# Longer row chunks in the channel mix, another way to turn the inverse row sums, and a re-tuned instruction order, in a top-k attention and channel-mix kernel

## The chip, the core and the metric

The kernel runs on one core of a Trainium2 chip. The metric is device time in microseconds of one launch. Before the change the median of three runs is 1353.63 us (1351.79 to 1354.52).

## What is computed

For 8 batches, 8 heads, 576 positions and a head size of 64, attention keeps for each row only the scores that reach the row's 32nd largest one, and normalises their exponentials by the row's sum plus 1e-9. The 4608 rows of 512 attention outputs then go through a channel mix with a gate:

```python
kth = np.partition(scores, -top_k, axis=-1)[..., -top_k:-top_k + 1]
scores = np.where(scores >= kth, scores, -1000000000.0)
attn = np.exp(scores - np.max(scores, axis=-1, keepdims=True))
attn = attn / (np.sum(attn, axis=-1, keepdims=True) + 1e-09)
x = np.matmul(attn, v)                       # then laid out as (8, 576, 512)
xk = mu_k * x + (1.0 - mu_k) * x_prev        # x_prev is x one row earlier, zeros for the first
xr = mu_r * x + (1.0 - mu_r) * x_prev
k = np.maximum(xk @ w_k, 0.0)                # 512 -> 1024
out = 1.0 / (1.0 + np.exp(-(xr @ w_r))) * (k * k @ w_v)   # gate 512 -> 512, value 1024 -> 512
```

Everything is float32. The channel mix keeps its accuracy by splitting each operand into a high and a low part of a faster format, so every product there is three matmuls (high by high, high by low, low by high).

## The kernel before

**Attention.** The work is cut into 288 tiles of 128 query rows by 576 keys: 32 pairs of heads (a batch and two heads), nine tiles each, of which the ninth holds the last 64 rows of both heads. A tile is scored on TensorE (L878, L882), copied to SBUF on ScalarE (L887), and its top 24 scores are found on VectorE, in seven pieces of 82 or 83 columns (L891, L893, L896). ScalarE's sign (L911), GpSimd's product (L913) and VectorE (L914, L916) find the 32nd score. ScalarE takes the exponential (L919); VectorE masks it and sums the rows in one pass (L922). TensorE then transposes the tile (L928, L937), ScalarE copies the transposes out (L930, L939), and TensorE multiplies by the values (L959, L961).

**Inverse row sums.** Four tiles of a pair form a unit (the ninth tile is a unit of its own), so there are 64 units of four tiles and 32 of one. When the last tile of a unit is masked, VectorE adds 1e-9 to the unit's row sums in place in SBUF (`inv`, L967) and takes the reciprocal (`inv2`, L968). The reciprocals stand one per partition, and they are needed along the free axis. TensorE does that turn with ordinary float32 matmuls: the reciprocal, broadcast to 64 columns, is the stationary operand and an identity the moving one (`turni`, L975), four matmuls for a unit of four tiles and two for a unit of one. The trace shows each of these as two instructions. ScalarE copies the result from PSUM to the tile `ri` (L981, L985), and VectorE multiplies the unit's sums by it into `xT`, the input of the channel mix (`place`, L992, L994).

**Channel mix.** The 4608 rows are taken in 22 chunks: 14 of 256 rows and 8 of 128 (the list `SIZES`). For each chunk GpSimd and ScalarE build the mixed inputs. Then TensorE computes the hidden layer (8 blocks of 128 hidden units, 4 pieces of the inner dimension, 3 products: 96 matmuls in the chunk, whose moving operand has as many columns as the chunk has rows), the gate (12 matmuls of 512 columns for each tile of up to 128 rows) and the value (24 matmuls of 512 columns for each such tile). Lines L597, L598 and L599 are the three products of one helper that serves all of these.

**PSUM.** Four banks, the `rot` tiles, take turns for everything that TensorE hands to another engine: transposed queries, keys and tiles, the inverse's turn, the hidden layer, the gate and the value. Two banks hold the scores and, at their outer ends, the unit's sums; the last two hold the exponentials and small tables.

**Order.** Every engine runs a list in order. The lists are made by a planner in the kernel (`Plan.run`), a list scheduler: each operation has a cost and a latency in nanoseconds, written by hand beside it, a key (its tile number plus an offset of its kind from `OFF`), and the tiles that it reads and writes. The planner walks through time, gives each engine the operation with the lowest key among those that can start within `NEAR` of the first, and grants a PSUM bank with the first operation that touches it. It knows extra costs on TensorE for going from one kind of work to another (`SWITCH`, `LEAVE`). Keys of the channel mix follow from the chunk's rows, `LAG`, `STEP`, `GATE` and `VALUE`. The emitted program is that list; at run time engines wait for one another by semaphores.

**Start.** VectorE, ScalarE and GpSimd first also turn the weights, which come as float64, into their high and low parts (L1158 to L1167), between the first attention tiles. The first matmul of the channel mix starts at 133.9 us.

Of the kernel before, what the change touches and what calls it, by code (L numbers as in the profile page):

```python
# [12 lines left out]
U32 = mybir.dt.uint32  # L13
AF = mybir.ActivationFunctionType
# [23 lines left out]
OFF = dict(kt=-7.052, kq=-6.285, rest=-4.016, v=-5.966, v8=-9.546, tk=-5.123, ck=-4.93, tq=-4.175, cq=-3.66, tr=-3.125, cr=-1.859, zero=7.516,  # L38
           score=-0.127, score8=0.064, keep=0.192, cand=1.258, best=1.414, drop=1.347, under=2.182, nb=-0.455, count=2.757, below=0.194, eighth=2.792,
           nine=1.785, exps=3.38, mask=2.98, turn=4.142, et=4.225, turnl=4.186, el=3.09, weigh=3.203, inv=2.807, inv2=4.903, turni=1.271, ri=4.531,  # L40
           place=4.604, lowest=26.228, ranks=3.686, mu=-1.636, nmu=1.291, changek=0.194, sharek=1.657, addk=-4.799, xhk=-4.813, xlk=-5.803,
           changer=-5.066, sharer=-4.564, addr=-3.661, xhr=-2.482, xlr=-2.503, hidden=0.91, relu=-0.32, sq=0.517, r2=-0.381, hl=-0.874, gate=2.195,
           gexp=1.225, ga=0.235, ln=1.619, inv1=1.333, newton=-1.097, value=0.746, scaled=-2.837, gated=-1.729, store=1.13, w=4.163, wabs=-1.596,
           wclamp=-0.639, wshift=-2.64, wsign=-0.217, wexp=-0.626, wfine=-1.896, whi=0.301, wmul=1.745, wsub=2.282, wlo=-0.346)
# [11 lines left out]
NEAR = dict(PE=128, ACT=137, DVE=15, POOL=110, SP=236)  # L56
# [82 lines left out]
class Plan:  # L139
# [53 lines left out]
    def run(self):  # L193
# [57 lines left out]
        while left:  # L251
            best = None
            for lane in lanes:
# [11 lines left out]
                t, item = min(((t, item) for t, item in able if t <= first + NEAR[lane]), key=lambda x: (x[1][0].key, x[1][0].n))  # L265
# [50 lines left out]
def topk_attention_channel_mix(ctx: ExitStack, tc: tile.TileContext, q, k, v, mu_k, mu_r, w_k, w_v, w_r, out):  # L316
# [448 lines left out]
    def attend(plan, visits, X, pair_sums):  # L765
# [8 lines left out]
        for p, (b, hp, part) in enumerate(visits):  # L774
# [84 lines left out]
            for i in part:  # L859
# [451 lines left out]
```

## Time and profile before

| | |
|---|---|
| median of three runs | 1353.63 us |
| the profiled execution's own time | 1351.31 us |
| its span, first to last instruction | 1349.5 us |
| busy: TensorE matmul | 1266.5 us, 94% |
| busy: VectorE | 1183.4 us, 88% |
| busy: ScalarE | 1148.0 us, 85% |
| busy: GpSimd | 986.7 us, 73% |
| mean granted TensorE clock | 0.969 of 2.4 GHz |

PE is TensorE, DVE VectorE, ACT ScalarE, POOL GpSimd. The profile counts a matmul as busy from its start to its modelled end, and matmuls overlap in the pipeline: one takes about 280 ns and the next can start 110 ns later. What a matmul costs its engine is therefore read from the distance between two starts in the timeline, not from its duration.

### The profile page before, as it was taken

How to read it: one execution, taken by the hardware profiler on the slowest of the kernel's cores; microseconds unless marked ns; L12 is line 12 of the kernel's file. 1: busy time of each engine (PE TensorE's matmuls, PEld its weight loads, DVE VectorE, ACT ScalarE, POOL GpSimd, SP SyncE). 2: the span in 40 equal slices, each digit the busy share in tenths (PEclk: the TensorE clock that was granted, in tenths of full speed). 3: DMA queues.
4: the chain of work that ended last, by engine and by line, in shares of the span. 5: the costliest groups of instructions: out<-in, count | busy, mean ns of one | idle time of the engine just before them, and what ended most of it. 6: DMA issues, size and time to landing. Idle time of an engine off the chain costs nothing.

```text
span 1349.5 us, 33121 instructions
## 1 busy us (share of the span) xinstructions
PE 1266.5 (94%) x10417; PEld 971.0 (72%) x10417; DVE 1183.4 (88%) x6220; ACT 1148.0 (85%) x2552; POOL 986.7 (73%) x858
## 2 busy tenths in 40 slices
PE   6566999999999989999999999999999999999996
PEld 3344777777777867777777777777877777777985
DVE  7999999998899899999899999999999999996000
ACT  7788899988899799989899899989799899987342
POOL 4998977766777568767688686867688687868584
PEclk9666999999999999999999999999999999999999
DMA  6532223223112121211221112111211213221000
GB/s 177 145 98 79 48 55 74 53 67 72 47 35 49 35 55 38 53 40 46 48 49 42 49 42 49 40 50 31 57 45 34 56 43 76 52 59 45 20 15 25
DMA packets 223386, 73.96 MB, mean 55 GB/s; under 512 B 216033, under 2 KB 216033, under 8 KB 223201
## 3 DMA queue, kind: packets, MB, share of 16 engines
q1 hardware_dynamic: 222656, 71.62, 21.5%
q8 instruction: 85, 1.39, 0.4%
q14 instruction: 101, 0.82, 0.2%
q10 hardware_dynamic: 544, 0.13, 0.0%
HBM read 62.26 MB, written 9.44 MB: 53 GB/s over the span
## 4 chain that ended last, share of the span: by engine, by line
PE 54%; DVE 30%; ACT 9%; issue 2%; POOL 2%; SPq 0%; DMA 0%; DVEq 0%; ACTq 0%; POOLq 0%
PE rot L597 9%; PE rot L599 9%; PE rot L598 9%; DVE cand L891 7%; PE ps L878 7%; PE rot L928 6%; DVE E L922 6%; PE ps L959 5%; DVE top L914 4%; PE rot L975 3%; DVE top L893 2%; DVE cand L896 2%; PE rot L831 2%; ACT sc L887 2%; ACT sg L911 2%
## 5 line engine op out<-in xcount | busy, mean ns | idle before, releaser
L913 POOL TENSOR_TENSOR sg<-sc,sg 128x576 f32<-128x576 f32 x288 | 408.0, 1419 | 217.3 <-ACT sg L911 214.0
L891 DVE MAX8 cand<-sc 128x8 f32<-128x82 f32 (+1 forms) x2016 | 406.3, 233 | 8.4 <-ACT sc L887 7.4
L911 ACT ACTIVATE sg<-sc,seen 128x576 f32<-128x576 f32 x288 | 224.5, 780 | 23.5 <-DVE seen L903 20.2
L922 DVE SCALAR_TENSOR_TENSOR E<-sc,seen,se 128x576 f32<-128x576 f32 x288 | 231.2, 803 | 1.4 <-ACT se L919 0.8
L919 ACT ACTIVATE se<-sc,seen 128x576 f32<-128x576 f32 x288 | 215.7, 749 | 13.6 <-DVE E L922 9.0
L914 DVE MAX8 top<-sg 128x8 f32<-128x576 f32 x288 | 216.0, 750 | 9.7 <-POOL sg L913 9.1
L878 PE MATMUL ps<-K,qs 64*128 64x288 f32 x1024 | 202.7, 474 | 18.8 <-ACT sc L887 17.7
L928 PE MATMUL rot<-ident,E 128*128 128x128 f32 x1152 | 186.1, 286 | 30.9 <-DVE E L922 14.1
L887 ACT ACTIVATE sc<-ps 128x576 f32<-128x576 f32 x288 | 187.1, 650 | 26.7 <-PE ps L878 17.3
L597 PE MATMUL rot<-xh,wk 128*128 128x256 f32 (+1 forms) x704 | 204.6, 291 | 1.1 <-DVE eb L1127 1.1
L599 PE MATMUL rot<-xh,wk 128*128 128x256 f32 (+1 forms) x704 | 196.2, 279 | 0.0
L598 PE MATMUL rot<-xl,wk 128*128 128x256 f32 (+1 forms) x704 | 196.0, 278 | 0.0
L928 PEld LDWEIGHTS rot<-ident,E 128*128 128x128 f32 x1152 | 132.6, 145 | 79.9 <-DVE E L922 21.6
L893 DVE MAX8 top<-cand 128x8 f32<-128x56 f32 x864 | 179.8, 208 | 4.2
L930 ACT ACTIVATE et<-rot 128x512 f32<-128x512 f32 x288 | 171.7, 598 | 4.8 <-PE rot L928 4.4
L959 PE MATMUL ps<-et,v 128*64 128x128 f32 x2048 | 146.8, 285 | 0.3 <-ACT et L930 0.2
L597 PEld LDWEIGHTS rot<-xh,wk 128*128 128x128 f32 x704 | 134.8, 191 | 7.5 <-issue 5.0
L959 PEld LDWEIGHTS ps<-et,v 128*64 128x64 f32 x2048 | 116.6, 141 | 30.6 <-issue 16.1
L598 PEld LDWEIGHTS rot<-xl,wk 128*128 128x128 f32 x704 | 134.0, 190 | 0.2
L599 PEld LDWEIGHTS rot<-xh,wk 128*128 128x128 f32 x704 | 133.6, 190 | 0.0
L878 PEld LDWEIGHTS ps<-K,qs 64*128 64x128 f32 x1024 | 80.4, 192 | 65.0 <-issue 28.5
L1096 POOL TENSOR_TENSOR r<-r 128x512 f32<-128x512 f32 (+1 forms) x88 | 77.9, 886 | 63.2 <-ACT hh L1094 56.5
(103 smaller groups left out, 2895.3 us busy)
## 6 DMA issues: line engine op xcount, KB each, us to landing
kt<-in_k SPq DMA_DIRECT2D x192, 72.0 KB, 2.2
v<-in_v SPq DMA_DIRECT2D x92, 128.0 KB, 2.5
kq<-in_q SPq DMA_DIRECT2D x80, 128.0 KB, 2.5
out<-eb SPq DMA_DIRECT2D x36, 256.0 KB, 2.1
kq<-in_q SPq DMA_DIRECT2D x94, 64.0 KB, 2.1
stage<-in_moe_w_k SPq DMA_DIRECT2D x8, 512.0 KB, 4.7
vu<-in_v SPq DMA_DIRECT2D x32, 128.0 KB, 2.4
stage<-in_moe_w_v SPq DMA_DIRECT2D x8, 512.0 KB, 3.7
```

What stands on the lines that cost most here:

```text
L597: nc.tensor.matmul(ps, lhsT=sh, rhs=mh, start=first, stop=False)
L598: nc.tensor.matmul(ps, lhsT=sh, rhs=ml, start=False, stop=False)
L599: nc.tensor.matmul(ps, lhsT=sl, rhs=mh, start=False, stop=last)
L878: nc.tensor.matmul(ps.t[:, e * HS:(e + 1) * HS], lhsT=P.qs[j].t[h, c * 128:(c + 1) * 128], rhs=P.K.t[h, j], start=True, stop=True)
L891: lambda T=T, c=c: nc.vector.max(T.cand.t[:, 8 * c:8 * c + 8], T.sc.t[:, CUTS[c]:CUTS[c + 1]]), reads=[T.sc], writes=[(T.cand, c)])
L911: lambda T=T, sn=sn: nc.scalar.activation(T.side.t, T.sc.t, AF.Sign, bias=sn(T, 1), scale=-BELOW, accum_out=T.top.t[:, TOPK:TOPK + 1]),
L913: plan.op(POOL, "below", n, 1375, 1430, lambda T=T: nc.gpsimd.tensor_mul(T.side.t, T.sc.t, T.side.t), reads=[T.sc], writes=[T.side])
L914: plan.op(DVE, "eighth", n, 660, 754, lambda T=T: nc.vector.max(T.top.t[:, 24:32], T.side.t), reads=[T.side], writes=[(T.top, 3)])
L919: plan.op(ACT, "exps", n, 667, 754, lambda T=T, pe=pe, sn=sn: nc.scalar.activation(pe.t, T.sc.t, AF.Exp, bias=sn(T, 0), scale=SCALE), read ...
L922: lambda T=T, U=U, pe=pe, sn=sn: nc.vector.scalar_tensor_tensor(T.e(), T.sc.t, sn(T, 2), pe.t, op0=OP.is_ge, op1=OP.mult, accum_out=U.rs.t ...
L928: nc.tensor.transpose(pt.t[:, c * 128:(c + 1) * 128], E.t[:, o + c * 128:o + (c + 1) * 128], ident)
L959: nc.tensor.matmul(pa[hs[j]], lhsT=vs[j][:, c, :], rhs=ms[c][j], start=(c == 0), stop=False)
```

## The change

The rows of the channel mix are cut into 19 chunks: fifteen of 256 rows, then 192, 256, 192 and 128. A chunk of 192 rows has a tile of 128 rows and one of 64.

The 1e-9 is added into PSUM instead of in place, and the reciprocal is read from there. GpSimd spreads each reciprocal over 64 columns (128 in a unit of one tile) into `ri`, and TensorE turns that with one or two transposes in place of two or four matmuls. The `rot` bank that takes the turn's result is now the same tile that takes the sum, so it is held from `inv` on. ScalarE's copy and VectorE's product stay as they were.

The planner's numbers are replaced: all offsets in `OFF`, `STEP`, `GATE`, `VALUE`, `NEAR` and others; several costs (hidden matmuls never under 111.7 ns, the weights' `wexp` 850 in place of 400, `ln` 650 in place of 537); more kinds of switch on TensorE; and `BONUS`, which shifts the key of a TensorE operation by the kind of work that came before it. `SPREAD` is "POOL", so the branches for ScalarE are not taken.

```diff
-SIZES = [256, 256, 128, 128, 256, 128] + [256, 256, 128, 256, 256] * 2 + [256, 256, 128, 128, 256, 128]
+SIZES = [256] * 15 + [192, 256, 192, 128]
-LAG, STEP, WAT, WSTEP, GATE, VALUE, PACE = 10.41, 16.746, 0.641, 1.281, 8.0, 12.488, -2.0
+LAG, STEP, WAT, WSTEP, GATE, VALUE, PACE = 10.41, 15.734, 0.542, 1.309, 7.28, 13.747, -2.0
-CANDS, BESTS = 0.062, 0.068
+CANDS, BESTS = 0.078, 0.41
-NEAR = dict(PE=128, ACT=137, DVE=15, POOL=110, SP=236)
+NEAR = dict(PE=158, ACT=176, DVE=0, POOL=131, SP=28)
+SPREAD, PLACE2 = "POOL", 340
...
-                t, item = min(((t, item) for t, item in able if t <= first + NEAR[lane]), key=lambda x: (x[1][0].key, x[1][0].n))
+                t, item = min(((t, item) for t, item in able if t <= first + NEAR[lane]), key=lambda x: (x[1][0].key + BONUS.get((mode, x[1][0].mode), 0.0), x[1][0].n))
...
-                    plan.op(DVE, "inv", n, 55, 150, lambda U=U: nc.vector.tensor_scalar(U.rs.t[:, :U.w], U.rs.t[:, :U.w], 1e-9, None, op0=OP.add), writes=[U.rs])
-                    plan.op(DVE, "inv2", n, 76, 170, lambda U=U: nc.vector.reciprocal(U.rs.t[:, :U.w], U.rs.t[:, :U.w]), writes=[U.rs])
-                                nc.tensor.matmul(pr.t[h, u * 128:(u + 1) * 128], lhsT=s.to_broadcast([128, 64]), rhs=ident, start=True, stop=True)
+                    plan.op(DVE, "inv", n, 60, 155, lambda U=U, pr=pr: nc.vector.tensor_scalar(pr.t[:, :U.w], U.rs.t[:, :U.w], 1e-9, None, op0=OP.add), reads=[U.rs], writes=[pr])
+                    plan.op(DVE, "inv2", n, 76, 170, lambda U=U, pr=pr: nc.vector.reciprocal(U.rs.t[:, :U.w], pr.t[:, :U.w]), reads=[pr], writes=[U.rs])
+                    each = 64 if i < 8 else 128
...
+                        to, r = U.ri.t[:, :w * each].rearrange("p (w d) -> p w d", w=w), U.rs.t[:, :w, None].to_broadcast([128, w, each])
+                            nc.gpsimd.tensor_scalar(to, r, 1.0, 1.0, op0=OP.mult, op1=OP.mult)
...
+                        for u in range(m):
+                            nc.tensor.transpose(pr.t[:, u * 128:(u + 1) * 128], U.ri.t[:, u * 128:(u + 1) * 128], ident)
...
-                    piece("hidden", key(f + e), 12 * (10.7 + n * 0.418), hid, [xh, xl, *[(X.w["k"], (i, f // 4)) for i in range(HP)]], [ph])
+                    piece("hidden", key(f + e), 12 * max(111.7, 10.7 + n * 0.418), hid, [xh, xl, *[(X.w["k"], (i, f // 4)) for i in range(HP)]], [ph])
```

## Rows read from the trace of the kernel before

**Rows 1.** The page: busy time of each engine with its share of the span and its instructions, and the shares of the engines in the chain of work that ended last.
```profile
PE 1266.5 (94%) x10417; PEld 971.0 (72%) x10417; DVE 1183.4 (88%) x6220; ACT 1148.0 (85%) x2552; POOL 986.7 (73%) x858
...
PE 54%; DVE 30%; ACT 9%; issue 2%; POOL 2%; SPq 0%; DMA 0%; DVEq 0%; ACTq 0%; POOLq 0%
```

**Rows 2.** The windows view: five stretches of the span. After the stretch and its length stand the busy times of PE, PEld (weight load), DVE, ACT and POOL with their instructions, then the granted TensorE clock, the DMA engines' share and GB/s.
```profile
0.00:70.00 70.00, 44.04 (x230) 26.86 (x232) 61.82 (x251) 51.40 (x106) 46.70 (x47) 0.76 0.60 158
70.00:240.00 170.00, 145.19 (x1156) 105.96 (x1157) 167.43 (x833) 150.77 (x332) 140.28 (x112) 0.87 0.29 72
240.00:1200.00 960.00, 939.76 (x8010) 720.35 (x8010) 909.99 (x4937) 870.61 (x1945) 701.12 (x601) 1.00 0.20 48
1200.00:1260.00 60.00, 59.42 (x534) 48.48 (x532) 36.70 (x191) 40.55 (x98) 37.55 (x37) 1.00 0.20 51
1260.00:1349.00 89.00, 78.06 (x496) 69.30 (x494) 7.51 (x13) 34.61 (x75) 61.02 (x64) 0.97 0.05 17
```

**Rows 3.** Groups of instructions by line and shape, TensorE: busy time and mean duration of one, idle time before. "128x256" is a chunk of 256 rows.
```profile
L928 PE MATMUL rot<-ident,E 128*128 128x128 f32 x1152 | 186.1, 286 | 30.9 <-DVE E L922 14.1 <-DVE top L893 4.3 <-ACT wv L1164 3.6
L597 PE MATMUL rot<-xh,wk 128*128 128x256 f32 x448 | 133.5, 298 | 1.1 <-DVE eb L1127 1.1
L597 PE MATMUL rot<-wv,hh 128*128 128x512 f32 x288 | 122.2, 424 | 0.0
L597 PE MATMUL rot<-xh,wk 128*128 128x128 f32 x256 | 71.1, 278 | 0.0
L597 PE MATMUL rot<-wr,xh 128*128 128x512 f32 x144 | 61.6, 428 | 0.1
L975 PE MATMUL rot<-ident,rs 128*64 128x128 f32 x640 | 56.6, 289 | 14.2 <-DVE rs L968 8.9 <-DVE top L893 1.4 <-DVE least L1001 1.3
```

**Rows 4.** Timeline of TensorE: start in the span, time from first start to last end, instructions. First hidden matmuls of 256 columns, from the first of a piece on; then value matmuls of 512 columns; then hidden matmuls of 128 columns. In each gap stand only more matmuls of the same kind: 7 between 1220.05 and 1221.00, 22 between 1265.61 and 1270.97, 43 between 1320.13 and 1325.05.
```profile
1219.61 0.36 PE L597 MATMUL rot<-xh,wk 128*128 128x256 f32 x1
1219.81 0.28 PE L598 MATMUL rot<-xl,wk 128*128 128x256 f32 x1
1220.05 0.28 PE L597 MATMUL rot<-xh,wk 128*128 128x256 f32 x1
...
1221.00 0.28 PE L599 MATMUL rot<-xh,wk 128*128 128x256 f32 x1
...
1265.61 0.40 PE L597 MATMUL rot<-wv,hh 128*128 128x512 f32 x1
...
1270.97 0.39 PE L599 MATMUL rot<-wv,hl 128*128 128x512 f32 x1
...
1320.13 0.28 PE L597 MATMUL rot<-xh,wk 128*128 128x128 f32 x1
...
1325.05 0.28 PE L599 MATMUL rot<-xh,wk 128*128 128x128 f32 x1
```

**Rows 5.** Timeline of TensorE around the inverse's turn (L975) and around transposes (L928, L937).
```profile
701.39 0.66 PE L975 MATMUL rot<-ident,rs 128*64 128x128 f32 x8 [0.80 <-DVE rs L968]
701.98 0.66 PE L928 MATMUL rot<-ident,E 128*128 128x128 f32 x4
...
709.49 0.60 PE L928 MATMUL rot<-ident,E 128*128 128x128 f32 x4
710.02 0.76 PE L878 MATMUL ps<-K,qs 64*128 64x288 f32 x4
...
1223.25 0.28 PE L599 MATMUL rot<-xh,wk 128*128 128x256 f32 x1
1223.37 0.60 PE L928 MATMUL rot<-ident,E 128*128 128x128 f32 x4
1223.80 0.27 PE L937 MATMUL rot<-ident,E 128*128 128x128 f32 x1
...
1225.21 0.28 PE L599 MATMUL rot<-xh,wk 128*128 128x256 f32 x1
1225.42 0.66 PE L975 MATMUL rot<-ident,rs 128*64 128x128 f32 x8
1225.90 1.04 PE L959 MATMUL ps<-et,v 128*64 128x128 f32 x16
```

**Rows 6.** Groups by line and shape, VectorE: the sum with 1e-9 of four and of one column, and the reciprocal of four.
```profile
L967 DVE TENSOR_SCALAR rs<-rs 128x4 f32<-128x4 f32 x64 | 32.8, 513 | 0.0
L968 DVE RECIPROCAL rs<-rs 128x4 f32<-128x4 f32 x64 | 10.3, 160 | 0.0
L967 DVE TENSOR_SCALAR rs<-rs 128x1 f32<-128x1 f32 x32 | 4.5, 140 | 0.0
```

**Rows 7.** Groups by line and shape, GpSimd: the product for the 32nd score, the gate's scalar operation of 512 columns, and a product of 256 columns.
```profile
L913 POOL TENSOR_TENSOR sg<-sc,sg 128x576 f32<-128x576 f32 x288 | 408.0, 1419 | 217.3 <-ACT sg L911 214.0 <-PE rot L599 0.7
L1112 POOL TENSOR_SCALAR eb<-eb 128x512 f32<-128x512 f32 x36 | 69.1, 1920 | 7.3 <-ACT eb L1111 4.8
L1096 POOL TENSOR_TENSOR r<-r 128x256 f32<-128x256 f32 x32 | 19.7, 614 | 33.5 <-ACT hh L1094 31.7 <-PE rot L937 1.2 <-PE rot L599 0.6
```

**Rows 8.** Timeline of VectorE: the sum with 1e-9 of one unit, and the reciprocal that follows it.
```profile
715.28 0.22 DVE L967 TENSOR_SCALAR rs<-rs 128x4 f32<-128x4 f32 x1
...
719.20 0.17 DVE L968 RECIPROCAL rs<-rs 128x4 f32<-128x4 f32 x1
```

More of the change, by code (lines that the diff above doesn't have):

```diff
@@ L37 @@
 BIG = 3.0e38
[L38 to L44, printed above, removed]
@@ L45 @@
-CANDS, BESTS = 0.062, 0.068
-LAG, STEP, WAT, WSTEP, GATE, VALUE, PACE = 10.41, 16.746, 0.641, 1.281, 8.0, 12.488, -2.0
+OFF = dict(kt=-7.011, kq=-6.835, rest=-7.805, v=-6.026, v8=-9.812, tk=-4.608, ck=-4.01, tq=-4.295, cq=-5.669, tr=-2.503, cr=-5.25, zero=7.982,
+           score=-0.504, score8=-2.241, keep=-0.323, cand=3.327, best=-1.159, drop=-0.827, under=-0.596, nb=-0.484, count=2.034, below=1.029,
+           eighth=2.875, nine=4.624, exps=2.951, mask=3.076, turn=3.921, et=4.228, turnl=3.656, el=1.141, weigh=3.297, inv=-0.082, inv2=5.091,
+           turni=1.833, ri=3.642, place=5.157, lowest=22.268, ranks=1.808, mu=-4.015, nmu=5.336, changek=7.504, sharek=-2.362, addk=-8.89, xhk=-4.232,
+           xlk=-11.512, changer=-0.97, sharer=-0.964, addr=4.74, xhr=-2.376, xlr=-5.331, hidden=0.557, relu=-1.816, sq=1.525, r2=-1.905, hl=-3.093,
+           gate=2.058, gexp=4.068, ga=2.473, ln=-2.445, inv1=2.025, newton=-3.534, value=0.69, scaled=-3.676, gated=-1.387, store=6.538, w=5.489,
+           wabs=-2.2, wclamp=0.087, wshift=-2.193, wsign=0.267, wexp=0.551, wfine=-3.489, whi=1.685, wmul=0.236, wsub=-2.316, wlo=1.183, spread=2.732)
@@ new lines, in attend, with spread @@
+                    plan.op(DVE, "inv2", n, 76, 170, lambda U=U, pr=pr: nc.vector.reciprocal(U.rs.t[:, :U.w], pr.t[:, :U.w]), reads=[pr], writes=[U.rs])
+                    each = 64 if i < 8 else 128
+                    wide = each * w
+                    def spread(U=U, w=w, each=each):
+                        to, r = U.ri.t[:, :w * each].rearrange("p (w d) -> p w d", w=w), U.rs.t[:, :w, None].to_broadcast([128, w, each])
+                        if SPREAD == "POOL":
+                            nc.gpsimd.tensor_scalar(to, r, 1.0, 1.0, op0=OP.mult, op1=OP.mult)
+                        else:
+                            nc.scalar.activation(to, r, AF.Copy)
@@ L976, in attend, with turn_i @@
+                    if SPREAD == "POOL":
+                        plan.op(POOL, "spread", n, 60 + 1.45 * wide, 60 + 1.45 * wide, spread, reads=[U.rs], writes=[U.ri], mode="TS")
+                    else:
+                        plan.op(ACT, "spread", n, 50 + 0.835 * wide, 165 + 0.835 * wide, spread, reads=[U.rs], writes=[U.ri])
                     m = 2 if i < 8 else 1
-                    plan.op(PE_, "turni", n, 114 * m, 114 * m + 197, turn_i, reads=[U.rs], writes=[pr, (U.ri, "held")], mode="W")
+                    def turn_i(U=U, pr=pr, m=m):
+                        for u in range(m):
+                            nc.tensor.transpose(pr.t[:, u * 128:(u + 1) * 128], U.ri.t[:, u * 128:(u + 1) * 128], ident)
@@ L979, in out_ri @@
+                    plan.op(PE_, "turni", n, 109 * m, 109 * m + 200, turn_i, reads=[U.ri], writes=[pr], mode="T")
                     def out_ri(U=U, pr=pr, i=i):
```

36 lines of the change are left out of this document (19 added, 17 removed).

## The prediction

> **What bounds the kernel now.** I read the page's shares first [rows 1], then the windows [rows 2], then single instructions. The page alone would not decide: TensorE is busy 94% of the span and VectorE 88%, and the chain that ended last is 54% TensorE and 30% VectorE. The windows show that they limit different stretches. From 0 to 240 us VectorE leads: at 70 to 240 us it is busy 167.4 of 170 us while TensorE is granted 0.87 of its clock and works 145. From 240 to 1200 us TensorE leads, 939.8 of 960 us (98%), with VectorE close behind at 910.0 (94.8%). After 1260 us only the channel mix is left: VectorE works 7.5 of 89 us, TensorE 78. So nearly 1100 of 1350 us are paced by TensorE, and an edit is priced by what it takes from TensorE's queue. Durations mislead there, so the price of a matmul is the distance between starts [rows 4, 5].
>
> **Longer chunks.** Hidden matmuls of 256 columns start (1221.00 - 1220.05) / 8 = 0.119 us apart, those of 128 columns (1325.05 - 1320.13) / 44 = 0.112 us [rows 4]. Half the columns save 6%: a matmul of 128 columns is nearly as dear as one of 256. Rows 3 count 448 and 256 of each of the three products, thus 1344 and 768 now: 1344 x 0.119 + 768 x 0.112 = 159.9 + 86.0 = 245.9 us. The 19 new chunks need 96 each: 16 x 96 = 1536 of 256, 192 of 192 and 96 of 128 columns. For 192 columns I take the middle, 0.115 (its bounds are the other two, 1 us in all): 182.8 + 22.1 + 10.8 = 215.7 us. That is 30 us less.
>
> Against it stands a tile more. Two chunks of 192 rows have four tiles where 384 rows needed three, and a tile of 64 rows streams 512 columns like a full one. Gate and value are 36 matmuls at (1270.97 - 1265.61) / 23 = 0.233 us [rows 4], 8.4 us. There are also three chunks' 24 fewer pieces of the hidden layer and six more of gate and value; entering a piece costs 1219.81 - 1219.61 - 0.12 = 0.08 us [rows 4], so 18 x 0.08 = 1.4 us at most. I take 1, because some pieces follow one another. Sum for TensorE: -30 + 8 - 1 = -23 us, with bounds -20 and -24. ScalarE and GpSimd lose three chunks' overheads and gain one tile's (GpSimd's is 1.92 us [rows 7]); both have idle time beside it, so I count nothing, and a few us if that cover goes.
>
> **Turning the inverses.** Now: a unit of four tiles takes eight passes. Followed by the values it occupies 1225.90 - 1225.42 = 0.48 us, followed by a transpose 701.98 - 701.39 = 0.59 [rows 5]. Entry from a hidden matmul costs 1225.42 - 1225.21 = 0.21 us where the next hidden matmul would have come after 0.12, thus 0.09 more. So 0.57 to 0.68 us. New: five transposes follow a hidden matmul without delay (1223.37 - 1223.25 = 0.12), and four take 1223.80 - 1223.37 = 0.43 us, 0.108 each. Leaving transposes for scores costs 710.02 - 709.49 - 0.43 = 0.10 [rows 5]. So two transposes cost 0.22 to 0.32, and a unit saves 0.25 to 0.46 us. I take 0.31, toward the lower end, because the values follow most often. The 32 units of one tile go from four passes to one transpose: half of the passes, the same entry, so 0.33 against 0.21 with the values behind, and up to 0.47 against 0.11; I take 0.2. 64 x 0.31 + 32 x 0.2 = 26 us; the bounds are 64 x 0.25 + 32 x 0.12 = 20 and 64 x 0.46 + 32 x 0.36 = 41.
>
> **The 1e-9 through PSUM.** In place, the sum of four columns takes 0.513 us, of one column 0.140 [rows 6], and three more columns can't be 0.37 us of arithmetic; most of it must be a wait. With the output in PSUM I take 0.15, between the single column's 0.140 and the reciprocal's 0.160; the upper bound is 0.513 as now. So VectorE loses 64 x 0.36 = 23 us, or nothing. From 240 us on it is not the bound, so this goes into the sum as nothing. But it decides whether VectorE can follow a faster TensorE, below.
>
> The Trainium skill (SBUF — State Buffer, Who interferes with whom) says that a VectorE scalar operation in a two-port mode and a GpSimd instruction hold one pair of ports exclusively, so that the later waits out the whole of the other, and (VectorE: DVE Perf Modes, Why PSUM operands drop a tier) that an operand in PSUM excludes that mode. By that rule the new sum never waits and VectorE is 23 us lighter; by the row alone it may be no lighter. The four-column mean, 0.513 us, agrees with such a wait; no row here writes it to PSUM.
>
> **Spreading on GpSimd.** No row shows it. The nearest of its kind is the gate's scalar operation, 1.92 us for 512 columns, thus 0.96 for 256; a product of 256 columns takes 0.61 [rows 7]. Below these it could be an instruction of 0.14 us as on VectorE. I take 0.65 and half of that for 128 columns: 64 x 0.65 + 32 x 0.33 = 52 us, bounds 11 and 77. GpSimd is busy 987 of 1349.5 us, and 217 us of its idle time stand before the product L913, waiting for ScalarE [rows 7]. So I count nothing for its time. But its queue is in order: while the spread waits for the reciprocal, L913 (1.42 us) of the next tile stands behind it, and VectorE waits for that. If the cover goes, 52 us.
>
> **The new order.** Every offset changes, so no row can be followed to its new place. I count it as zero: TensorE keeps 98% in the middle stretch. The bounds: 20 us are not busy from 240 to 1200 us and 51 from 0 to 240 [rows 2], and a better order could win perhaps 25 of these; a worse one could lose as much.
>
> **Sum.** 1351.3 (the profiled execution: span 1349.5 and 1.8 around it) - 23 - 26 = 1302.3 us. The median of the runs lies 2.3 above that execution, so I predict 1304 us. It asks much of VectorE. In the middle stretch its work falls by 23 x 960/1349 = 16 to 894 us, and the stretch itself by 49 x 960/1349 = 35 to 925: 96.6% busy, against 98.5% in its busiest stretch [rows 2]. That fits, narrowly.
>
> **The rivals.** 1. *VectorE shares the bound.* Savings are worth only what their engine holds of the chain: 49 x 0.54 + 23 x 0.30 = 33 us [rows 1], 1320 us. For it: 94.8% in the stretch that is to shrink. Against it: 98.5% was reached.
>
> 2. *Slower: the turn's PSUM bank is held too long.* The bank is now taken by the sum with 1e-9, not by the turn. In the rows the reciprocal follows 715.28 to 719.20, 3.9 us later [rows 8]; then come up to 1.42 us behind L913, 0.65 for the spread, and the turn. So one of four banks is gone some 6 us of the 17 that four tiles last (the attention's 288 tiles end near 1237, where VectorE's 36.7 us from 1200 on run out [rows 2]: 1237/288 x 4). Place: TensorE waiting for a bank before a transpose or a hidden piece. Price: 1 us for each of 96 units gives 1304 + 96 = 1400 us; from 49/96 = 0.51 us per unit on the change loses. Against it: the planner grants banks itself, and so sees this hold.
>
> 3. *The clock.* TensorE is granted 1.00 in the middle stretch and 0.87 before [rows 2]. If the lighter queue fell back to 0.87 from 240 to 1200 us, those 925 us would take up to 925/0.87 = 1063: 1304 + 138 = 1442 us. For it: less matmul work and more waiting. Against it: 1152 transposes [rows 3] stand in a stretch at 1.00, and the new ones fill 64 x 0.22 + 32 x 0.11 = 18 us. The Trainium skill (TensorE: Matmul & The Clock Gate, Part 4: PE-mode transpose) says that transposes don't count as the activity that keeps the clock up, and here 640 passes that do become 160 that don't. No run here separates the two kinds of pass; the rows at 1.00 hold both, so the chance stays small.
>
> 4. *The order itself wins.* 25 us of TensorE's idle time return: 1279 us.
>
> 5. *It doesn't do what it says*: the saved matmul time only turns into waits, because the re-timed lists fit the chip no better: 1351 to 1354.
>
> **How the numbers follow.** Forecast (1288 to 1315) 0.49; rival 1 (1315 to 1342) 0.25; rival 4 (below 1288) 0.13; rival 5 0.04; rival 2 0.06; rival 3 0.03. The range 1274 to 1342 leaves out 2, 3, 5 and the lowest few hundredths of 4. A measurement of this kernel can't tell less than about 0.2% from no change, 2.7 us. Faster by more: 0.49 + 0.25 + 0.13 = 0.87. Within: 0.03, most of rival 5. Slower: rivals 2 and 3 and the rest of 5, 0.10.
>
> **What the next profile would show.** Right: hidden matmuls in three shapes, 1824 in all, at the same distances; 160 transposes where 640 passes were; the four-column sum at about 0.15 us; TensorE still at 97% or more between the start-up and the tail, at clock 1.00, and VectorE at 96 to 97%. Wrong: VectorE at 98% and TensorE with gaps that it ends (rival 1); TensorE's gaps ended by ScalarE's copies, ahead of work that needs a `rot` bank (rival 2); a granted clock below 1.00 after 240 us (rival 3). If the spread takes over 1 us or GpSimd ends VectorE's gaps, its price of nothing was wrong.

## The result and the profile after

The changed kernel takes **1313.7 us** (median of 4 runs, 1312.52 to 1314.63), against 1352.9 for the kernel before in the same comparison: a ratio of 0.971, 95% interval 0.9692 to 0.9726. That is 39 us less. The forecast was 1304, 49 us less; the result lies in its band of 1288 to 1315, at the upper edge.

The page of the changed kernel: busy time of each engine, TensorE's granted clock in 40 slices, and the engines' shares of the chain that ended last.

```profile
PE 1226.5 (93%) x9685; PEld 930.3 (71%) x9685; DVE 1162.4 (89%) x6222; ACT 1135.4 (86%) x2495; POOL 1018.3 (78%) x908
...
PEclk9576999999999799999999999999999999999998
...
PE 42%; DVE 35%; ACT 14%; POOL 5%; issue 3%; DMA 0%; DVEq 0%; SPq 0%; ACTq 0%; POOLq 0%
```

Against [rows 1] TensorE lost 40 us of busy time and VectorE 21, and GpSimd gained 32. In the chain TensorE fell from 54% to 42% and VectorE rose from 30% to 35%. One slice in the middle of the clock's row holds a 7, which the row of the kernel before does not have. The middle window of the changed kernel, in the columns of [rows 2]:

```profile
240.00:1200.00 960.00, 940.17 (x7712) 713.86 (x7712) 926.93 (x5111) 890.23 (x1971) 750.19 (x665) 0.99 0.21 50
```

In the stretch from 240 to 1200 us VectorE rose from 94.8% to 96.6%, and TensorE stayed at 98%. But the same 960 us hold another part of the work in each kernel, so I cut both by work instead: from the start of the mask of the 49th attention tile (L922 before, L924 after) to that of the 277th, and from there to the end. First the kernel before, then the changed one, columns as above.

```profile
248.20:1193.20 945.00, 924.76 (x7908) 709.17 (x7906) 895.16 (x4867) 856.14 (x1911) 689.46 (x588) 1.00 0.20 48
1193.20:1349.50 156.30, 144.28 (x1072) 122.88 (x1066) 50.97 (x232) 81.49 (x189) 102.46 (x105) 0.98 0.12 33
```

```profile
247.70:1147.00 899.30, 880.55 (x7213) 668.32 (x7212) 872.94 (x4824) 836.72 (x1846) 703.77 (x624) 0.99 0.21 50
1147.00:1312.90 165.90, 153.63 (x1097) 125.65 (x1095) 57.08 (x258) 88.55 (x197) 114.67 (x109) 0.98 0.12 32
```

This says where the time went. The first 48 tiles take as long as before (247.7 against 248.2 us). The 228 tiles of the middle take 45.7 us less. The tail takes 9.6 us **more**, with 9.4 us more TensorE work in it. And the middle's 45.7 us are, on VectorE, 22.2 us less work (895.16 - 872.94) and 23.4 us less idling (49.8 before, 26.4 after); on TensorE they are 44.2 us less work and 1.5 us less idling. Both engines are now within 3% of the stretch. From this alone one can't tell which of them sets the pace; the experiments do.

The groups that the change made, TensorE first, columns as in [rows 3], then VectorE and GpSimd, as in [rows 6, 7]:

```profile
L599 PE MATMUL rot<-xh,wk 128*128 128x256 f32 x512 | 154.2, 301 | 0.0
L599 PE MATMUL rot<-xh,wk 128*128 128x192 f32 x64 | 17.9, 280 | 0.0
L601 PE MATMUL rot<-xh,wk 128*128 128x128 f32 x32 | 8.8, 275 | 0.0
L988 PE MATMUL rot<-ident,ri 128*128 128x128 f32 x160 | 36.5, 295 | 7.2 <-POOL ri L977 6.6
...
L969 DVE TENSOR_SCALAR rot<-rs 128x4 f32<-128x4 f32 x64 | 10.2, 160 | 0.0
L969 DVE TENSOR_SCALAR rot<-rs 128x1 f32<-128x1 f32 x32 | 5.0, 158 | 0.5 <-ACT et L932 0.5
...
L977 POOL TENSOR_SCALAR ri<-rs 128x256 f32<-128x256 f32 x64 | 26.0, 406 | 12.1 <-DVE rs L970 8.5 <-DVE cand L893 1.3 <-DVE nine L918 0.7
L977 POOL TENSOR_SCALAR ri<-rs 128x128 f32<-128x128 f32 x32 | 9.5, 297 | 13.3 <-DVE xT L1006 8.8 <-DVE rot L969 2.9 <-DVE seen L905 1.1
```

The counts are the forecast ones: 3 x (512 + 64 + 32) = 1824 hidden matmuls, 160 transposes for 640 passes. The sum of four columns takes 0.160 us (0.513 before), the spread 0.406 and 0.297.

One unit can be followed on the timeline of all engines of the changed kernel (start, time, engine):

```profile
491.54 1.41 POOL L915 TENSOR_TENSOR sg<-sc,sg 128x576 f32<-128x576 f32 x1
...
491.90 0.16 DVE L969 TENSOR_SCALAR rot<-rs 128x4 f32<-128x4 f32 x1
...
492.24 0.17 DVE L970 RECIPROCAL rs<-rot 128x4 f32<-128x4 f32 x1
...
492.92 0.40 POOL L977 TENSOR_SCALAR ri<-rs 128x256 f32<-128x256 f32 x1
...
493.37 0.44 PE L988 MATMUL rot<-ident,ri 128*128 128x128 f32 x2
...
493.66 0.39 PE L599 MATMUL rot<-xh,wk 128*128 128x256 f32 x1
...
494.01 0.28 PE L601 MATMUL rot<-xh,wk 128*128 128x256 f32 x1
...
494.19 0.41 ACT L993 ACTIVATE ri<-rot 128x256 f32<-128x256 f32 x1
...
494.48 0.28 PE L599 MATMUL rot<-xh,wk 128*128 128x256 f32 x1
```

The inverse is ready at 492.41; the spread starts at 492.92, when GpSimd's product L915 ends. The two transposes take 493.66 - 493.37 = 0.29 us, and four hidden matmuls of 256 columns (494.48 - 494.01) / 4 = 0.118 us each. The PSUM bank of the turn is held from 491.90 to the end of ScalarE's copy, 494.60: 2.7 us here, 4.8 in the mean of the 96 units (each from the start of its L969 to the end of its L993 or its second L997). Hidden matmuls of 192 columns, six from start to start on TensorE's timeline, cost (1195.22 - 1194.55) / 6 = 0.112 us, no more than those of 128 [rows 4]:

```profile
1194.55 0.28 PE L599 MATMUL rot<-xh,wk 128*128 128x192 f32 x1
...
1195.22 0.27 PE L599 MATMUL rot<-xh,wk 128*128 128x192 f32 x1
```

### The profile page after: what moved, and what is told of

Same layout as the page of the kernel before. It is cut to its first block, busy times and chain, and to the rows that moved or that the text cites. A ratio compares the mean times of both kernels' runs of the same rounds, so it can differ in the third digit from the quotient of the medians.

```text
span 1312.9 us, 31609 instructions
## 1 busy us (share of the span) xinstructions
PE 1226.5 (93%) x9685; PEld 930.3 (71%) x9685; DVE 1162.4 (89%) x6222; ACT 1135.4 (86%) x2495; POOL 1018.3 (78%) x908
## 3 DMA queue, kind: packets, MB, share of 16 engines
q1 hardware_dynamic: 222672, 71.62, 22.2%
## 4 chain that ended last, share of the span: by engine, by line
PE 42%; DVE 35%; ACT 14%; POOL 5%; issue 3%; DMA 0%; DVEq 0%; SPq 0%; ACTq 0%; POOLq 0%
DVE cand L893 9%; PE rot L599 7%; DVE E L924 7%; PE rot L600 7%; PE rot L601 7%; PE ps L880 6%; DVE top L916 5%; PE ps L961 4%; PE rot L930 4%; DVE top L895 4%; DVE cand L898 4%; ACT sg L913 3%; ACT sc L889 3%; ACT se L921 2%; PE rot L833 2%
## 5 line engine op out<-in xcount | busy, mean ns | idle before, releaser
L915 POOL TENSOR_TENSOR sg<-sc,sg 128x576 f32<-128x576 f32 x288 | 409.9, 1425 | 166.8 <-ACT sg L913 164.8
L893 DVE MAX8 cand<-sc 128x8 f32<-128x82 f32 (+1 forms) x2016 | 397.2, 232 | 6.8 <-ACT sc L889 6.0
L924 DVE SCALAR_TENSOR_TENSOR E<-sc,seen,se 128x576 f32<-128x576 f32 x288 | 231.2, 803 | 1.3 <-ACT se L921 0.6
L599 PE MATMUL rot<-xh,wk 128*128 128x256 f32 (+2 forms) x608 | 180.8, 297 | 0.0
L601 PE MATMUL rot<-xh,wk 128*128 128x256 f32 (+2 forms) x608 | 170.6, 281 | 0.0
L600 PE MATMUL rot<-xl,wk 128*128 128x256 f32 (+2 forms) x608 | 170.5, 280 | 0.0
L961 PE MATMUL ps<-et,v 128*64 128x128 f32 x2048 | 152.5, 290 | 1.1 <-ACT et L932 0.9
L961 PEld LDWEIGHTS ps<-et,v 128*64 128x64 f32 x2048 | 118.6, 143 | 44.1 <-issue 32.1
L599 PE MATMUL rot<-wv,hh 128*128 128x512 f32 (+1 forms) x296 | 127.2, 430 | 0.1
L599 PEld LDWEIGHTS rot<-xh,wk 128*128 128x128 f32 x608 | 116.9, 192 | 3.1 <-issue 1.7
L601 PE MATMUL rot<-wv,hl 128*128 128x512 f32 (+1 forms) x296 | 116.9, 395 | 0.0
L600 PE MATMUL rot<-wv,hh 128*128 128x512 f32 (+1 forms) x296 | 116.8, 395 | 0.0
```

What stands on the lines that cost most here:

```text
L599: nc.tensor.matmul(ps, lhsT=sh, rhs=mh, start=first, stop=False)
L600: nc.tensor.matmul(ps, lhsT=sh, rhs=ml, start=False, stop=False)
L601: nc.tensor.matmul(ps, lhsT=sl, rhs=mh, start=False, stop=last)
L893: lambda T=T, c=c: nc.vector.max(T.cand.t[:, 8 * c:8 * c + 8], T.sc.t[:, CUTS[c]:CUTS[c + 1]]), reads=[T.sc], writes=[(T.cand, c)])
L915: plan.op(POOL, "below", n, 1375, 1430, lambda T=T: nc.gpsimd.tensor_mul(T.side.t, T.sc.t, T.side.t), reads=[T.sc], writes=[T.side])
L924: lambda T=T, U=U, pe=pe, sn=sn: nc.vector.scalar_tensor_tensor(T.e(), T.sc.t, sn(T, 2), pe.t, op0=OP.is_ge, op1=OP.mult, accum_out=U.rs.t ...
```

## The experiments

Ten of the 49 us did not come. The theory that I started with (A) was a **hole**: SIZES ended a chunk at row 1152 = 2 x 576 before, which is the end of the second batch; now the chunk of rows 1024 to 1279 lies across it and must wait for rows of the third batch's last head pair. TensorE has no channel-mix matmul from 427.7 to 471.8 us, its longest pause in the changed kernel (21.3 us before). The rival is that TensorE's savings count only in part, because VectorE holds the pace too. Times below are medians of at least 4 runs, ratios are to the kernel before in the same comparison (1351.6 to 1352.4 us). Differences to the changed kernel are of medians of different comparisons, so some 1.5 us of them mean nothing.

**Undoing one part at a time.** Four kernels, each the changed one but for this:

```diff
--- e1_aligned: chunks that end at row 1152, and no half-filled tile
-SIZES = [256] * 15 + [192, 256, 192, 128]
+SIZES = [256] * 4 + [128] + [256] * 13 + [128]
--- e2_sizes_old: the old chunks
+SIZES = [256, 256, 128, 128, 256, 128] + [256, 256, 128, 256, 256] * 2 + [256, 256, 128, 128, 256, 128]
--- e3_order_old: the old OFF, CANDS, BESTS, LAG to PACE, SWITCH, NEAR and durations
+BONUS = {}
--- e4_turn_old: the old turn of the inverses, the sum in place
+plan.op(DVE, "inv", n, 55, 150, ... nc.vector.tensor_scalar(U.rs.t[:, :U.w], U.rs.t[:, :U.w], 1e-9, None, op0=OP.add), writes=[U.rs])
+nc.tensor.matmul(pr.t[h, u * 128:(u + 1) * 128], lhsT=s.to_broadcast([128, 64]), rhs=ident, start=True, stop=True)
```

> The changed kernel with SIZES = [256]*4 + [128] + [256]*13 + [128]: a chunk ends at row 1152, the end of batch 1, and no chunk has a tile of 64 rows. Theory A (the missing 10 us are a hole: the chunk of rows 1024 to 1279 needs rows of batch 2 and leaves TensorE without mix work from 427.7 to 471.8 us): the longest pause between mix matmuls falls from 44 us to about 25, the clock stays at 1.00 there, 8 us go with the extra tile and 8 to 15 us with the hole: 1291 to 1298 us. Theory B (VectorE holds the savings back evenly): only the tile's 8 us or less, 1305 to 1311 us.

Measured: **1302.77 us**, ratio 0.9640 (0.9624 to 0.9656), 11 us below the changed kernel. The windows from 420 to 480 us, first of the changed kernel, with a narrower one in it, then of e1:

```profile
420.00:480.00 60.00, 50.66 (x405) 34.84 (x405) 57.60 (x338) 51.19 (x113) 29.38 (x29) 0.89 0.21 49
...
438.00:445.00 7.00, 6.51 (x36) 4.65 (x36) 6.61 (x42) 5.04 (x12) 3.19 (x3) 0.51 0.03 6
```

```profile
420.00:480.00 60.00, 55.93 (x463) 42.32 (x465) 54.77 (x306) 51.19 (x114) 35.31 (x33) 0.99 0.20 49
...
246.30:1147.20 900.90, 887.10 (x7288) 672.42 (x7286) 871.58 (x4850) 842.19 (x1864) 708.72 (x629) 1.00 0.21 50
1147.20:1301.10 153.90, 139.27 (x986) 116.75 (x984) 50.71 (x230) 80.55 (x175) 107.22 (x102) 0.97 0.13 35
```

The hole is there and can be mended: TensorE does 463 instead of 405 matmuls in these 60 us, and its granted clock is 0.99 instead of 0.89. In the hole, with attention work alone and waits between, the clock fell to half (0.51 in the 7 us from 438 on, the lower of its two levels, 1.2 GHz): four score matmuls that took 0.76 us at 429.51 took 1.33 at 439.72. This is in TensorE's timeline of the changed kernel:

```profile
429.51 0.76 PE L880 MATMUL ps<-K,qs 64*128 64x288 f32 x4
...
439.72 1.33 PE L880 MATMUL ps<-K,qs 64*128 64x288 f32 x4
```

The longest pause in the mix fell from 44.0 to 24.9 us (458.1 to 483.1); the clock did not stay at 1.00 in it, but at 0.94 and 0.89 in the two 10 us from 470 on. But the gain does not show where the hole was. From the 49th to the 277th tile e1 needs 900.9 us, the changed kernel 899.3. In the hole VectorE had kept working (57.6 of 60 us) and attention ran ahead; what TensorE left undone, it did later. The whole gain is in the tail: 153.9 against 165.9 us, with 14.4 us less TensorE work. The missing half-filled tile is 8.4 us of that by the prediction's working, the mix that is no longer left over the other 6. 14.4 us of work brought 12.0 here, so the hole's share is about 5 us (an estimate; no run has the border without the tile). A is right in kind, but by this estimate explains only half of the ten that were missing.

> The changed kernel with the 22 old chunks. By the prediction's term alone 23 us more, 1337 us. Theory A: the new sizes earn 23 us of matmul time and give some 10 to 15 back in the hole, which the old sizes, with a border at row 1152, have only in its old length: 1322 to 1329 us. Theory B: VectorE is the bound with either, so less than 23 us comes back, at no particular place: 1325 to 1335 us, with the pauses as they are now.

Measured: 1329.9 us, 0.9840 (0.9824 to 0.9856). The new chunks are worth 16 us to the changed kernel, not 23. The time lies just above theory A's range and inside theory B's, but the longest pause, 27.2 us instead of 44.0, is as A had it. So this run does not choose between them.

> The changed kernel with the old planner numbers (offsets, STEP, GATE, VALUE, NEAR, switches, costs, no BONUS), new sizes, new turn. By the prediction the order is worth nothing: 1314 us within 5. If the re-tuned order had won and covered a loss elsewhere: 1325 us or more. If it lost the 10 us: 1304 us.

Measured: 1346.34 us, 0.9962 (0.9949 to 0.9974). The old planner's numbers cost 33 us in the new code. This was no zero. Cut by work as above, 17.7 us of it are lost before the 49th tile (it comes at 265.4 us instead of 247.7), 3 in the middle and 10 in the tail. The spread, which the old lists did not have, keeps its new offset (`spread=2.732`) among the old ones, as in e6 below, which starts just as slowly.

> The changed kernel with the old way to turn the inverses (sum in place, four or two matmuls, no spread). By the prediction's term 26 us more, 1340 us, and 23 us more VectorE work beside it. If the spread and the longer held bank cost TensorE waits, less: 1325 us. If VectorE has become the bound (theory B), its 23 us count too: 1345 us or more.

Measured: 1357.87 us, 1.0049 (1.0033 to 1.0066): 44 us above the changed kernel, and slower than before. With the turn and the sum as they were, longer chunks and a new order gain nothing at all. TensorE's 26 us alone don't explain that. VectorE's 23 beside them would (theory B), and so would an order that no longer fits the old turn; e7, e8 and e11 below tell these apart.

**One part alone on the old kernel, and the turn split in two.**

```diff
--- e5_sizes_only: the kernel before
+SIZES = [256] * 15 + [192, 256, 192, 128]
--- e6_turn_only: the kernel before with the new L969 to L1008; due times as they were, and for the new step
+spread=2.732
--- e7_order_only: the kernel before with the new OFF, CANDS, ..., NEAR, BONUS and durations
--- e8_sum_in_place: the changed kernel, planned anew with
-nc.vector.tensor_scalar(pr.t[:, :U.w], U.rs.t[:, :U.w], 1e-9, None, op0=OP.add), reads=[U.rs], writes=[pr])
+nc.vector.tensor_scalar(U.rs.t[:, :U.w], U.rs.t[:, :U.w], 1e-9, None, op0=OP.add), writes=[U.rs])
-nc.vector.reciprocal(U.rs.t[:, :U.w], pr.t[:, :U.w]), reads=[pr], writes=[U.rs])
+nc.vector.reciprocal(U.rs.t[:, :U.w], U.rs.t[:, :U.w]), writes=[U.rs])
```

> The kernel before with the new chunk sizes alone (old turn, old planner numbers). By the prediction's term 23 us less, 1329 us. Theory A (the border at row 1152 falls inside a chunk, and the mix pauses): a pause near 440 to 490 us longer than the 21 us of before, and a gain of 10 us or less: 1342 us or more.

Measured: 1348.56 us, 0.9978 (0.9967 to 0.9988), 3 us less. Theory A's sign came: the longest pause in the mix is 53.0 us (427.5 to 480.5). But the small total hides two large parts, as the cut by work shows:

```profile
250.30:1171.50 921.20, 889.36 (x7560) 674.86 (x7560) 892.74 (x4852) 841.47 (x1844) 668.13 (x540) 0.99 0.20 49
1171.50:1347.10 175.60, 164.47 (x1161) 134.83 (x1157) 54.17 (x241) 89.97 (x198) 119.03 (x108) 0.98 0.12 32
```

The middle is 24 us shorter than the 945.0 of before, with VectorE idling 28.5 us instead of 49.8; the tail is 19 us longer than 156.3, with 20 us more TensorE work left over for it; the start is 2 us longer.

> The kernel before with the new way to turn the inverses alone (old sizes, old planner numbers). By the prediction's term 26 us less, 1326 us, if TensorE is the bound; with VectorE's 23 us beside it perhaps 1320. If the longer held bank and the wait for GpSimd cost what the turn saves (rival 2): 1345 us or more.

Measured: 1354.99 us, 1.0022 (1.0013 to 1.0032), 3 us **more**, though VectorE and TensorE both have less to do. The trace shows one reason near the start: the timelines of GpSimd and of TensorE in e6.

```profile
161.84 2.75 POOL L915 TENSOR_TENSOR sg<-sc,sg 128x576 f32<-128x576 f32 x2
164.55 1.26 POOL L1094 TENSOR_TENSOR xl<-xm,xh 128x512 fp32r<-128x512 f32 x1
165.77 1.39 POOL L915 TENSOR_TENSOR sg<-sc,sg 128x576 f32<-128x576 f32 x1
167.13 0.40 POOL L977 TENSOR_SCALAR ri<-rs 128x256 f32<-128x256 f32 x1
...
167.59 0.69 PE L988 MATMUL rot<-ident,ri 128*128 128x128 f32 x2 [7.93 <-POOL ri L977]
```

A spread of 0.40 us stands in GpSimd's list behind a whole run of other work, and TensorE, in order too, stands 7.93 us before its two transposes. The 49th tile comes at 264.3 us instead of 248.2. That is the queue that the prediction named beside the spread; with due times made for the old code it is no longer covered. This stall is 8 of the 16 us; what made the others is not shown. From the 49th tile on e6 is 14 us **faster** than the kernel before: 931.1 us for the middle instead of 945.0, and a tail of 156.0 instead of 156.3. So the turn does earn something on the old lists, and a slow start takes it back.

```profile
264.30:1195.40 931.10, 912.53 (x7486) 696.44 (x7486) 882.86 (x4854) 854.04 (x1912) 718.29 (x666) 1.00 0.20 48
```

> The kernel before with the new planner numbers alone (old sizes, old turn). By the prediction 1352 us within 5. If a re-tuned order is worth something by itself, not only to the two edits: 1335 us or less. If it fits only the code that it was tuned for: 1355 us or more.

Measured: 1369.51 us, 1.0129 (1.0112 to 1.0146): the new order makes the old code 17.6 us slower. By the pages its VectorE is busy 21.3 us more (1204.7 against 1183.4), with the same work.

> The changed kernel with the 1e-9 added in place in SBUF, and everything else kept. The four-column sum goes back to about 0.5 us. By the prediction, that counts these 23 us of VectorE as nothing, 1314 us within 5; the bank is also held a little shorter. If VectorE paces the attention of the changed kernel: 10 to 23 us more, 1324 to 1337 us.

Measured: 1342.02 us, 0.9931 (0.9915 to 0.9948), **28 us** above the changed kernel. The sum of four columns took 0.663 us here. So this one instruction, which the prediction counted as nothing, is the largest gain on the path that follows.

These runs make a path from the old kernel to the new: new order +17.6 us (e7, from 1351.9), new chunks -11.6 (e4), new turn with the sum in place -15.9 (e8), the sum through PSUM -28.3 (the changed kernel). Alone on the old kernel, order, chunks and turn give +18, -3 and +3, the last two with gains of 24 and 14 us in the middle that the tail and the start take back.

**Which engine sets the pace?** Three kernels keep the changed kernel's instruction lists word for word and add work to one engine inside a step. The fourth does it to the kernel before.

```diff
--- e9_vector_more: the first of seven searches twice, in all 288 tiles
-lambda ...: nc.vector.max(T.cand.t[:, 8 * c:8 * c + 8], T.sc.t[:, CUTS[c]:CUTS[c + 1]])
+lambda ...: [nc.vector.max(T.cand.t[:, 8 * c:8 * c + 8], T.sc.t[:, CUTS[c]:CUTS[c + 1]]) for _ in range(2 if c == 0 else 1)]
--- e10_tensor_more: the last of four transposes of L930 twice, in all 288 tiles
-for c in range(NKC):
+for c in (*range(NKC), NKC - 1):
--- e11_sum_same_list: the sum in place as in e8, but with the bank still declared
+plan.op(DVE, "inv", ..., reads=[U.rs], writes=[pr])
--- e12_before_vector: the kernel before, the first search twice in every third tile
+[nc.vector.max(...) for _ in range(2 if c == 0 and T.i % 3 == 0 else 1)]
```

> The changed kernel, each engine's list as it is, with VectorE's first search of 82 columns done twice in every tile: 288 more operations that follow one another 0.145 us apart, 42 us of VectorE. If TensorE alone paces the attention (the prediction's reading): under 10 us more, 1324 us or less. If VectorE paces it in the changed kernel: 30 to 42 us more, 1344 to 1356 us.

> The changed kernel, each engine's list as it is, with one transpose of every tile done twice: 288 more at 0.109 us, 31 us of TensorE. If TensorE paces the attention: 25 to 31 us more, 1339 to 1345 us. If VectorE does: under 12 us more, 1326 us or less. If both limit, each in turn: this and the run with more VectorE work both land at about half.

> The changed kernel with the 1e-9 added in place and each engine's list as it is (the earlier run with the sum in place let the planner list anew). The four-column sum takes 0.5 to 0.65 us, 23 to 32 us more of VectorE. If VectorE paces the attention: 23 to 32 us more, 1337 to 1346 us. If the new list was what cost the earlier run its 28 us: under 10 us more, 1324 us or less.

> The kernel before, each engine's list as it is, with VectorE's first search of 82 columns done twice in every third tile: 96 more operations. The run with one in every tile of the changed kernel lengthened VectorE's busy time by 69.7 us, 0.24 us each, so 23 us here, as much as the 1e-9 in PSUM takes away. If TensorE paces the kernel before and VectorE has slack (the prediction's reading): 0 to 6 us more. If VectorE paces it already: 18 to 23 us more, about 1371 to 1376 us. Half of that if they take turns.

Measured: e9 1379.47 us, ratio 1.0201 (1.0184 to 1.0218); e10 1327.26, 0.9818 (0.9801 to 0.9835); e11 1341.37, 0.9923 (0.9906 to 0.9941); e12 1367.91, 1.0110 (1.0093 to 1.0127). By the pages, e9's VectorE was busy 1232.1 us, 69.7 more than in the changed kernel, and the time rose by 65.8: 94% of it. e11's VectorE was busy 32.1 us more, for 27.7: 86%. In e10 TensorE got 288 transposes at 0.108 us [rows 5], 31 us, for 13.6: 44%. This share is not measured like the others: TensorE's busy time rose by only 17.3 us (1243.8 against 1226.5), and 13.6 is 79% of that, while by the 42 us that its expectation counted e9 would come to 157%. By either measure VectorE's share is the larger, and TensorE's is far from nothing. And in the old kernel 20.9 us more of VectorE (1204.3 against 1183.4) cost 15.7: 75%.

The windows view from the 49th to the 277th tile, one fence each for e9, e10, e11 and e12:

```profile
259.80:1211.10 951.30, 889.11 (x7207) 666.89 (x7207) 924.62 (x5051) 840.36 (x1844) 704.01 (x624) 1.00 0.20 47
```

```profile
249.50:1158.50 909.00, 897.02 (x7442) 690.21 (x7441) 877.48 (x4825) 842.77 (x1846) 704.39 (x624) 1.00 0.21 50
```

```profile
252.70:1170.80 918.10, 886.22 (x7214) 669.22 (x7213) 894.24 (x4824) 838.12 (x1846) 705.04 (x624) 0.99 0.20 49
```

```profile
251.30:1210.50 959.20, 931.11 (x7906) 711.49 (x7904) 912.48 (x4942) 858.13 (x1911) 689.55 (x588) 1.00 0.20 47
```

Read the idle time of each engine, stretch less busy. VectorE idles 26.4 us in the changed kernel, 26.7 in e9, 23.9 in e11: nearly the same, however much work it has, so the stretch is as long as VectorE makes it. TensorE idles 18.7 us in the changed kernel, 62.2 in e9 and 31.9 in e11: it waits for whatever VectorE takes. With more TensorE work (e10) its idling falls only to 12.0, VectorE's rises to 31.5, and 24 us of transposes lengthen the stretch by 9.7. So VectorE holds the pace in the changed kernel, with TensorE close behind. In the old kernel VectorE idles 49.8 us, and 46.7 with e12's work: it held most of the pace there already.

The cause can be seen in one group of e11; below it stand the engines' shares in e10's chain:

```profile
L969 DVE TENSOR_SCALAR rs<-rs 128x4 f32<-128x4 f32 x64 | 40.4, 632 | 0.0
```

```profile
PE 75%; DVE 12%; ACT 6%; POOL 2%; issue 1%; DMA 0%; SPq 0%; DVEq 0%; ACTq 0%; POOLq 0%
```

The same instruction takes 0.632 us in place and 0.160 into PSUM, in the same lists. What it waits for stands in the timelines of GpSimd and VectorE, first of e11, then of the changed kernel:

```profile
622.25 1.41 POOL L915 TENSOR_TENSOR sg<-sc,sg 128x576 f32<-128x576 f32 x1
622.39 1.29 DVE L969 TENSOR_SCALAR rs<-rs 128x4 f32<-128x4 f32 x1
```

```profile
610.97 1.41 POOL L915 TENSOR_TENSOR sg<-sc,sg 128x576 f32<-128x576 f32 x1
611.14 0.15 DVE L969 TENSOR_SCALAR rot<-rs 128x4 f32<-128x4 f32 x1
```

Both sums start inside a GpSimd instruction. In place, the sum ends when that one has ended (623.68 and 623.66); into PSUM, it takes 0.15 us beside it. This holds over the traces. In the kernel before, 37 of the 64 sums of four columns took over 0.25 us, in e11 47: every one of them started inside a GpSimd instruction and ended 0.02 to 0.07 us after it. The 16 of before that started with GpSimd at rest, or within 0.06 us of its end, took 0.161 us at most. With the output in PSUM none of 64 took over 0.168, though 59 started inside a GpSimd instruction. Nor do sums of one column wait, and the reciprocal of the same four cells, in place too, takes 0.160 [rows 6]. A few sums in place did not wait (3 of before took 0.15 us beside an instruction with 0.87 us or more to run); why is not shown.

And the chain of e10 is 75% TensorE, although the 31 us of work added to TensorE made it only 13.6 us longer: with two engines this close, the chain's shares say through which the path happened to run, not what work on it is worth.

## Why the prediction was right, and where it was not

The time came out 10 us above the forecast, and the sum behind it was partly right by accident: two terms on TensorE were counted 17 to 21 us too high, one on VectorE 28 too low, and the order, counted as nothing, cost 18 on the path above. That these nearly cancel is luck.

**The step that failed** is "From 240 us on it is not the bound, so this goes into the sum as nothing", and before it "nearly 1100 of 1350 us are paced by TensorE, and an edit is priced by what it takes from TensorE's queue". I read it from 98% against 94.8% in [rows 2]. But a TensorE at 98% is one whose matmuls' ends are modelled and whose switches between kinds are covered by those ends ([rows 5]: the last transpose from 709.49 on ends at 710.09, after the scores have started at 710.02); e12 shows that VectorE's work in the old kernel cost 75% of its length. A second view could have warned me: what VectorE waited for. In the old kernel's waits of VectorE (us in all, times, longest), outside the two lines of the tail (L1126), little is left:

```profile
DVE rot L1126 <- ACT lb L1114: 58.9, 3, 29.2
DVE rot L1126 <- PE rot L599: 25.7, 5, 16.7
DVE top L914 <- POOL sg L913: 9.1, 13, 1.7
DVE cand L891 <- ACT sc L887: 7.4, 9, 2.2
DVE seen L903 <- PE se L961: 7.1, 8, 1.6
```

Not one entry outside the tail is above 9.1 us in some 1200. An engine that waits so little is not cheap.

**The 1e-9 through PSUM.** Its size was nearly right: 0.160 us against the 0.15 taken, so 64 x (0.513 - 0.160) = 23 us off VectorE, as worked out; its price was wrong, 28 us instead of 0. That it exceeds 23 is because the wait in place is no constant: 0.663 us in e8 and 0.632 in e11, so 64 x 0.47 = 30 us in the new order, where more of the sums start inside a GpSimd instruction (55 of 64 in e11, 48 in the kernel before). The Trainium skill (SBUF — State Buffer, Who interferes with whom; VectorE: DVE Perf Modes, Why PSUM operands drop a tier) gave the rule by which a result in PSUM does not wait for GpSimd, and the row now agrees: 0.160 us in the mean of the changed kernel's 64 units, 0.168 at most. The trace agrees on the other side too: each long sum in place ends with a GpSimd instruction, as shown above.

**Longer chunks.** The work was priced well: 0.118 us for 256 columns against 0.119, 0.112 for 192 columns against the 0.115 taken, so about 1 us less than the 215.7 worked out. Of the 23 us that this takes from TensorE 16 reached the time (e2). The tile more was priced well too (its matmuls start 0.231 us apart against the 0.233 taken), and was a real loss: without it and with the border at row 1152 the kernel is 11 us faster (e1). The prediction had no term for that border.

**Turning the inverses.** Two transposes cost 0.29 us in the row above, within the 0.22 to 0.32 worked out. (By the prediction's own terms a unit of one tile costs at most 0.24 + 0.11 + 0.09 = 0.44 us before, not 0.47, so its bound of 41 us is 40.) 26 us off TensorE were worth 15.9 (e4 to e8). Together, TensorE's 49 us were worth 11.6 (e7 to e4) or 16.2 (e2) and 15.9, thus 28 to 32, some three fifths.

**Spreading on GpSimd.** 0.406 and 0.297 us against 0.65 and 0.33, 35.5 us in all against 52; GpSimd's busy time rose by 32. Counting it as nothing held in the new order: the product L915's waits for ScalarE, 164.8 us, cover it, and TensorE's matmuls waited 6.6 us for the spread. The warning on the queue in order held too: in e6 it alone took 7.9 us in one place.

**The new order.** Counted as zero between -25 and 25. It is not a term that can be added: 18 us slower on the old code (e7), 33 us faster on the new (e3), of which 17.7 arise before the 49th tile.

**The rivals.** Rival 1, VectorE shares the bound, names the mechanism; its price by the chain's shares, 33 us, was short of the 39, since it put VectorE's 23 us at 0.30 where e11 gives 0.86. Its sign in the trace was to be "VectorE at 98% and TensorE with gaps that it ends"; VectorE stayed at 97% even in e9, so that threshold was wrong. Of the gaps it was right: TensorE's longest entry of the changed kernel's waits is for VectorE's masked scores.

```profile
PE rot L939 <- DVE E L924: 20.2, 7, 6.2
PE ps L880 <- ACT sc L889: 12.8, 21, 2.4
PE rot L988 <- POOL ri L977: 6.6, 9, 3.1
```

Rival 2, the bank held too long, did not happen: 4.8 us in the mean instead of 6, and no entry of 3 us or more among TensorE's waits is for the copies L993 and L997. With the sum in place the bank was held shorter, and the kernel was 28 us slower. Two separate banks were not tried. Rival 3, the clock, came in one place, the hole, at a price that e1 bounds; else it was 1.00 from 240 us to the tail. (The 1152 transposes that the prediction held against it are those of the whole run; 932 of them start between 240 and 1200 us.) The Trainium skill's rule that transposes don't count (TensorE: Matmul & The Clock Gate, Part 4: PE-mode transpose) changed nothing here: with 160 transposes for 640 passes the clock was 1.00 in the stretches from 480 to 1190 us. Rival 4, the order wins by itself, did not come: alone it lost 18 us (e7). Rival 5 is what e4 shows of a version without the turn.

The fastest version run is **e1, 1302.77 us**, 49 us below the kernel before: the same change with chunks that end where the batch ends.

## What to carry to other kernels

Where two engines are both above 94% busy in a stretch, price neither at nothing: double a small step of each in unchanged lists and see what share of it the time takes (here, of the rise in its busy time, 94% for VectorE and 79% for TensorE). Chunk borders belong where the data before them is complete; a chunk across a batch's end left a hole of 44 us in the mix. Due times tuned for one program are part of that program: taken alone to the old code they cost 18 us, left old in the new code 33. And a change that shortens the stretch you look at can lengthen the one after it: the longer chunks alone won 24 us in the middle and lost 19 in the tail.

## What the hardware showed that I had not expected

- A sum of four columns in place on VectorE took 0.51 to 0.66 us in the mean of different runs, because those that started inside a GpSimd instruction mostly ended only with it and took up to 1.4 us; those that met none took 0.16 at most. With one column it took 0.14 in the same kernels, and into PSUM both took 0.16, with GpSimd at work or not.
- A search of 82 columns done again at once into the same eight cells took (1232.1 - 1162.4) / 288 = 0.24 us of VectorE's busy time, as much as a search by itself (0.232). Three searches in a row into different cells take 0.52 us together on the timeline at 492.90, so (0.52 - 0.232) / 2 = 0.14 for each after the first. I had reckoned the doubled one at the latter.
- Matmuls of 192 columns start as close as those of 128, 0.112 us; those of 256 at 0.118. Between 192 and 128 columns nothing is saved.
- Attention alone, with its waits, did not keep TensorE's clock up in the hole (0.51 in 438 to 445 us), while from 480 to 1190 us, with the mix between, it stayed at 1.00.
